# Two layers of hedgehog attention and squared-ReLU MLP: attention weights paced by POOL's copies, more row tiles turned by way of DRAM and DVE, keys taken in another order

## The chip, the cores and the metric

One core of one Trainium2 chip runs the whole program. The metric is device time in microseconds (us) for one execution; less is better.

## The reference

Two equal layers over 2048 rows of 576 floats. Each layer is a linear attention with learned feature maps (32 heads of 18), then an MLP of width 4608 with a squared ReLU; both start with a layer norm and add to the residual. All is float32.

```python
pq = einsum("bhsd,hdf->bhsf", q, w_phi); pk = einsum("bhsd,hdf->bhsf", k, w_phi)
phi_q = concatenate([softmax(pq), softmax(-pq)], axis=-1)     # phi_k alike
kv = einsum("bhsf,bhsd->bhfd", phi_k, v); z = einsum("bhsf->bhf", phi_k)
o = einsum("bhqf,bhfd->bhqd", phi_q, kv) / (einsum("bhqf,bhf->bhq", phi_q, z)[..., None] + 1e-6)
A(x) = o.reshape(B, S, D) @ wo                                # q, k, v = x @ wqkv
B(x) = square(relu(x @ w1 + b1)) @ w2 + b2
x = x + A(layernorm(x)); x = x + B(layernorm(x))              # twice, same weights
```

## The kernel before

**Products.** Every float32 operand is split into a high and a low part (float32r), and a product is three matmuls: high by high, high by low, low by high. Weights are kept in DRAM in split form and loaded from there.

**Blocks.** The rows are taken in four blocks of 512 (four tiles t of 128). The MLP of a block runs over 36 chunks f of 128 hidden features. `hidden(f)` multiplies chunk f of w1 (tile h1, rows m_2h in the profile; one load of 640 KB) with the block's turned rows into a PSUM tile ph; `square(f)` lets ACT make relu and square (hr, L980 and L981) and DVE the split (hb, L984 and L985); `second(f-1)` multiplies the chunk before with w2 (tile s2, rows m_2s, 576 KB) into accumulators (L1000 and L992). h1 and s2 have two buffers each, so the load for chunk f+1 can start when chunk f-1 has been used. In layer 0 the blocks come in the order 3, 2, 0, 1; the profile calls them m_3, m_2, m_0 and m_1. The first one also splits the MLP weights and stores them.

**What is woven in.** `g_mlp` yields between its halves: slot 2f comes after hidden(f), slot 2f+1 after second(f-1). Into these slots `weave` puts the steps of a plan: `plan.put(at, order, call)` files a call under turn `at`, and turn k falls on slot 2k+1. The steps of a block in layer 0 are:

- `plan_attend` (L868): the rest of layer 0's attention for the next block (a_2 in m_3, a_0 in m_2, a_1 in m_0): queries, division, output projection with the weights "o" (tiles a_0o0h, a_0o0l and so on), norm and turn of its rows for the MLP.
- `plan_keys` (L1515): in m_2, m_0 and m_1 the keys and values of layer 1 for the block before (n_3 in m_2, then n_2 and n_0): norm of its rows, turn, `keys(t)` with the weights k (tiles w_3k0h, w_3k0l, w_3k1h, w_3k1l), `values(t)` with the weights v (w_3v...), softmax, and `add(t)`, which adds a tile's part of kv (L593; 128 matmuls of 36 columns for two tiles). These weights come as four pieces of 720 KB each, by `asked` (L302), which returns four calls that issue them.

**Turning rows.** A product needs rows with the features on partitions. `Norm.turn` (L375) does that with four TensorE transposes a tile into PSUM (L384), then a copy by ACT (L385) and a subtraction by DVE (L386); `Norm.rest` (L389) does the last 64 features, two tiles at a time (L393 to L395). `TripNorm` (L400) does it without TensorE for the tiles in `trips`: `store` puts the normed tile into DRAM (xrm, L419; with `tails` also the last 64 features, xrt, L422), `fetch` loads it back with its 32x32 blocks exchanged (L430, L432), both issued from ACT's queue, `flip` transposes inside the blocks on DVE, and `turn` splits it with ACT (L451) and DVE (L452). In before, a_2 takes this way with tiles 0 to 2 and without tails; the other attentions of a layer take it whole; the key blocks turn all four tiles on TensorE.

**Order.** The instructions of PE, ACT, DVE and POOL stand in the order in which the program writes them. SP, which issues nearly all loads (`nc.sync.dma_start`), stands in an order that the framework's scheduler makes. Each engine takes its queue strictly from the front: a load whose buffer isn't free yet holds back all loads behind it.

Of the kernel before, what the change touches and what calls it, by code (L numbers as in the profile page):

```python
# [15 lines left out]
NT = TB // P  # L16
# [5 lines left out]
def layers_kernel(  # L22
# [278 lines left out]

    def asked(which, name, tags=TAGS_A):  # L302

        pair, calls = [], []

        def ask(half, k):
            if k == 0:
                pair.append(piece_tiles(f"{name}{which}{half}", tags))
            for d, piece in moved(which, half, k, pair[half][k]):
                nc.sync.dma_start(piece, d)  # L310

        return pair, [lambda half=half, k=k: ask(half, k) for half in range(2) for k in range(2)]
# [12 lines left out]
    class Norm:  # L325
# [49 lines left out]
        def turn(self, t):  # L375
            name, dst, xn = self.name, self.dst, self.xn.pop(t)
            if t == 0:
                dst.update(xt_tiles(name))
# [18 lines left out]
    class TripNorm(Norm):  # L397
# [44 lines left out]
        def turn(self, t):  # L442
            if t not in self.trips:
                return super().turn(t)
            xn, dst = self.xn.pop(t), self.dst
            if t == 0:
                dst.update(xt_tiles(self.name))
# [420 lines left out]
    def plan_attend(plan, at, gap, layer, b, raws, dst, name, o, homes=None, queries=None, lead=1):  # L868
# [28 lines left out]
        for t in range(NT):  # L897
            plan.put(at + t - 1, 9, out.load, t)
        trips = range(NT if whole else NT - 1)
        norm = TripNorm(dst, f"{name}n", b, out.keep, trips, whole)  # L900
        more = 0 if queries else 2
        scales = [at + 1, at + 2, at + 3, at + 4 if whole else at + 5.5 + more]
        turns = [at + more + k for k in (4, 5, 6.5, 7)]
        for t in trips:
            plan.put(scales[t] + 0.5, -1, norm.store, t)
            plan.put(at + more + t + 2.5, -1, norm.fetch, t)
            plan.put(at + more + (3.5, 4.5, 6, 6.5)[t], -1, norm.flip, t)
        plan_norm(plan, norm, out.project, [at + t for t in range(NT)], scales, turns, [at + 5 + more, at + 7 + more])

    def g_mlp(layer, b, x, after, name, fresh, apart, final):  # L910
# [66 lines left out]
        def square(f):  # L977
# [6 lines left out]
            nc.vector.tensor_copy(hh, hr)  # L984
            nc.vector.tensor_sub(hl, hr, hh.bitcast(F32))  # L985
            parts[f] = (s2, hh, hl)

# [470 lines left out]
    def body():  # L1458
# [3 lines left out]
        for layer in range(2):  # L1462
            q1 = None
            ready, prev_rows, keep = {}, None, {}
            for i, b in enumerate(order):
# [11 lines left out]
                if prev_rows is not None:  # L1477
                    at = plan_keys(plan, prev_rows, i == NB - 1, keep)
                if i + 1 < NB:
                    nb, n2 = order[i + 1], f"a{layer}_{order[i + 1]}"  # L1480
                    if i or layer:
                        o = asked("o", n2, TAGS_C)
                    if i == 0:
                        plan_attend(plan, 1, 3, layer, nb, [other.raws[t] for t in range(NT)], nxt, n2, o,
                                    TAGS_C if layer else None)
                    elif layer == 0:
# [6 lines left out]
                        for n, call in enumerate(o[1]):  # L1493
                            plan.put(at + n, 9, call)
                        plan_attend(plan, at - 4.5, 2, layer, nb, raws2, nxt, n2, o, TAGS_A, take, 2)
                    else:
                        raws2, held = [], {}
# [16 lines left out]

    def plan_keys(plan, prev_rows, last, keep):  # L1515

        pb, done = prev_rows
        m = f"1_{pb}"
        xk, es, ks, vts = {}, {}, {}, {}
        plan_norm(plan, Norm(xk, f"n{m}"), lambda t: done[t], (0, 0, 1, 2), (1, 1, 2, 3), (2, 3, 4, 4.5), (3, 5), (3,))  # L1520
        (vw, vcalls), (kw, kcalls) = asked("v", f"w{m}"), asked("k", f"w{m}", TAGS_C)
        for n in range(4):
            plan.put(8 + n if last else 2 + n / 2, 9, vcalls[n])
            plan.put(n / 2, 9, kcalls[n])
        if not last:
            for n in range(4):
                plan.put(5 + n / 2, -1, lambda n=n: spill(pb, xk, [n]))

# [16 lines left out]

        for t in range(NT):
            plan.put(4 + t, 0, keys, t)
            plan.put(5 + t, 1, soft1, t)
            plan.put(6 + t, 2, soft2, t)
            if not last:  # L1550
                plan.put(4.5 + t, 0, values, t)
                plan.put(8.5 + t // 2 * 2, 3, add, t)
        if last:
# [27 lines left out]
```

## Time and profile before

| | |
|---|---|
| median of 3 runs | 2497.05 us (2494.74 to 2499.38) |
| the profiled execution | 2497.19 us |
| its span, first to last instruction | 2495.5 us |
| PE busy | 2478.5 us, 99% |
| DVE, ACT, POOL busy | 1260.1, 788.1, 189.4 us |
| moved by DMA | 545.07 MB, 218 GB/s on the average |

The 1.7 us between span and time lie around the instructions. An engine's row in the page is its busy time, its share of the span and its instructions. In a table of waits, a row names who waited for whom: us in total, how often, the longest. A row of a timeline begins with start and duration in us; "xN" is N instructions run together; brackets at its end hold the idle time before it and what ended it. A row of a chain is start, duration and what held the end back. Durations of neighbouring matmuls overlap, so the time that one takes on PE is read from start to start.

### The profile page before, as it was taken

Reading aid. Unit: us, or ns where it says so; the run is one execution under the profiler, and the core shown is the slowest. Engines: PE = TensorE matmul, PEld = TensorE weight load, DVE = VectorE, ACT = ScalarE, POOL = GpSimd, SP = SyncE. Lnnn points to the kernel's source line nnn. Section 1 sums busy time; section 2 is a strip of 40 time slices with the busy share of each in tenths; the row PEclk is TensorE's granted clock in tenths of the full one; section 3 lists DMA queues with packets and bytes.
Section 4 is the critical chain, followed back from the end, with each engine's and each line's share of the span. In section 5 each row is a group of like instructions: output and inputs, shape, how many; then the busy total and the mean of one; then the engine's idle time right before and its main releaser. Section 6 shows DMA issues by size and latency. Waiting matters only on the chain.

```text
span 2495.5 us, 37635 instructions
## 1 busy us (share of the span) xinstructions
PE 2478.5 (99%) x14968; PEld 2182.9 (87%) x14968; DVE 1260.1 (50%) x2214; ACT 788.1 (32%) x1439; POOL 189.4 (8%) x539
## 2 busy tenths in 40 slices
PE   9999999999999999999999999999999999999999
PEld 8999888888888888888888988888888888888887
DVE  6679885545744476455113776433453436442112
ACT  5444453422232223223213332413233222312212
POOL 4211100000200001000000011000110002000000
PEclk9999999999999999999999999999999999999999
DMA  9313698986767677684565248678576867676565
GB/s 321 98 54 92 243 315 266 310 315 205 259 229 271 217 206 273 216 298 146 195 199 182 92 141 263 209 217 291 186 257 204 261 219 246 217 230 230 194 199 171
DMA packets 214374, 545.07 MB, mean 218 GB/s; under 512 B 29006, under 2 KB 96814, under 8 KB 214198
## 3 DMA queue, kind: packets, MB, share of 16 engines
q1 hardware_dynamic: 163638, 500.44, 60.8%
q10 hardware_dynamic: 50560, 42.21, 5.3%
q8 instruction: 119, 1.95, 0.3%
q14 instruction: 57, 0.47, 0.1%
HBM read 439.20 MB, written 103.38 MB: 217 GB/s over the span
## 4 chain that ended last, share of the span: by engine, by line
PE 95%; DMA 2%; DVE 1%; ACT 1%; issue 1%; SPq 0%; ACTq 0%; DVEq 0%
PE m_1ph L975 9%; PE m_3ph L975 9%; PE m_0ph L975 9%; PE m_2ph L975 9%; PE m_1acc L1000 7%; PE m_3acc L1000 7%; PE m_2acc L1000 7%; PE m_0acc L1000 7%; PE m_1acc L992 2%; PE m_3acc L992 2%; PE m_2acc L992 2%; PE m_0acc L992 2%; PE a_0po L816 1%; PE a_2po L816 1%; PE kvp L593 1%; PE a_3po L816 1%
## 5 line engine op out<-in xcount | busy, mean ns | idle before, releaser
L975 PE MATMUL m_2ph<-a_2nh,m_2h 128*128 128x512 f32 x720 | 225.2, 394 | 1.2 <-ACT m_2hr L980 0.7
L975 PE MATMUL m_0ph<-a_0nh,m_0h 128*128 128x512 f32 x720 | 225.0, 394 | 1.3 <-ACT m_0hr L980 1.1
L1000 PE MATMUL m_3acc<-m_3s,m_3hb 128*128 128x448 f32 x864 | 189.3, 367 | 0.4 <-DVE m_3hb L984 0.4
L1000 PE MATMUL m_1acc<-m_1s,m_1hb 128*128 128x448 f32 x864 | 189.0, 367 | 0.3 <-PE m_1ph L975 0.3
L1000 PE MATMUL m_2acc<-m_2s,m_2hb 128*128 128x448 f32 x864 | 188.9, 367 | 0.0
L1000 PE MATMUL m_0acc<-m_0s,m_0hb 128*128 128x448 f32 x864 | 188.8, 367 | 0.0
L984 DVE CAST m_2hb<-m_2hr 128x512 fp32r<-128x512 f32 x72 | 31.2, 433 | 292.4 <-ACT m_2hr L981 292.3
L1000 PEld LDWEIGHTS m_1acc<-m_1s,m_1hb 128*128 128x128 f32 x864 | 161.9, 188 | 18.8 <-PE m_1ph L975 0.5
L1000 PEld LDWEIGHTS m_3acc<-m_3s,m_3hb 128*128 128x128 f32 x864 | 161.2, 188 | 17.8 <-PE m_3ph L975 0.6
L1000 PEld LDWEIGHTS m_2acc<-m_2s,m_2hb 128*128 128x128 f32 x864 | 161.6, 188 | 17.2
L1000 PEld LDWEIGHTS m_0acc<-m_0s,m_0hb 128*128 128x128 f32 x864 | 161.6, 188 | 17.2
L975 PEld LDWEIGHTS m_2ph<-a_2nh,m_2h 128*128 128x128 f32 x720 | 135.3, 188 | 32.7 <-ACT m_2hr L980 1.2
L975 PEld LDWEIGHTS m_0ph<-a_0nh,m_0h 128*128 128x128 f32 x720 | 135.2, 188 | 32.8 <-ACT m_0hr L980 1.5
L984 DVE CAST m_1hb<-m_1hr 128x512 fp32r<-128x512 f32 x72 | 30.7, 427 | 258.8 <-ACT m_1hr L981 258.8
L980 ACT ACTIVATE m_2hr<-m_2ph,b1t 128x512 f32<-128x512 f32 x72 | 49.6, 689 | 339.1 <-PE m_2ph L975 327.4
L980 ACT ACTIVATE m_1hr<-m_1ph,b1t 128x512 f32<-128x512 f32 x72 | 49.6, 689 | 319.1 <-PE m_1ph L975 309.1
L980 ACT ACTIVATE m_0hr<-m_0ph,b1t 128x512 f32<-128x512 f32 x72 | 49.6, 689 | 317.2 <-PE m_0ph L975 288.6
L984 DVE CAST m_0hb<-m_0hr 128x512 fp32r<-128x512 f32 x72 | 31.5, 438 | 229.0 <-ACT m_0hr L981 229.0
L984 DVE CAST m_3hb<-m_3hr 128x512 fp32r<-128x512 f32 x72 | 31.7, 440 | 173.6 <-ACT m_3hr L981 173.6
L980 ACT ACTIVATE m_3hr<-m_3ph,b1t 128x512 f32<-128x512 f32 x72 | 49.6, 689 | 219.3 <-PE m_3ph L975 209.2
L975 PE MATMUL m_3ph<-t0onh,m_3h 128*128 128x512 f32 (+1 forms) x380 | 112.9, 384 | 0.6 <-ACT t0onh L385 0.5
L975 PE MATMUL m_1ph<-t1onh,m_1h 128*128 128x512 f32 (+1 forms) x380 | 112.4, 382 | 0.8 <-ACT t1onh L385 0.5
(2050 smaller groups left out, 5734.9 us busy)
## 6 DMA issues: line engine op xcount, KB each, us to landing
m_2h<-dw SPq DMA_DIRECT2D x72, 640.0 KB
m_0h<-dw SPq DMA_DIRECT2D x72, 640.0 KB
m_1h<-dw SPq DMA_DIRECT2D x72, 640.0 KB
m_2s<-dw SPq DMA_DIRECT2D x72, 576.0 KB
m_0s<-dw SPq DMA_DIRECT2D x72, 576.0 KB
m_1s<-dw SPq DMA_DIRECT2D x72, 576.0 KB
dw<-m_3h SPq DMA_DIRECT2D x36, 640.0 KB
m_3h<-dw SPq DMA_DIRECT2D x36, 640.0 KB
```

The source lines that it names most:

```text
L593: nc.tensor.matmul(po[32 * q : 32 * q + 32, :, j], vt[:, h * VW : h * VW + 32], e[:, :, h * DH : (h + 1) * DH], start=not stay, stop=True, ...
L816: nc.tensor.matmul(pt[:, :HP], a, m[:w, g], start=(g == 0 and k == 0), stop=(g == NG - 1 and k == 2))
L975: nc.tensor.matmul(ph[:, cols], a, m, start=(k == 0), stop=(k == 3 * KC + 1))
L980: nc.scalar.activation(hr, ph, AF.Relu, bias=b1t[:, f : f + 1])
L984: nc.vector.tensor_copy(hh, hr)
L992: nc.tensor.matmul(acc[KC], a, m, start=(f == 0 and k == 0), stop=(f == NF - 1 and k == 2))
L1000: nc.tensor.matmul(acc[t][:, :R], a[:, rows], m, start=(f == 0 and k == 0), stop=(f == NF - 1 and k == 2))
```

## The change

1. `asked` gets a switch `paced`. With it, POOL first copies one element of the newest hr (`beat["now"]`, set at the end of `square`) into the piece's tile, and only then is the piece's load issued: the load overwrites that element, so it must come behind the copy, and the copy behind hr. It is used for k, v and "o" in layer 0's blocks (32 copies; of "o" only the pieces of 126 partitions are held so).
2. `plan_attend` sends all four tiles and the tails by way of DRAM also for a_2.
3. `plan_keys` turns tiles 0 and 1 by way of DRAM (store at turn 2, fetch at 3 and 4, flip at 4.5 and 5.5, turn at 5 and 6), tiles 2 and 3 on TensorE at turns 2 and 3, and all tails on TensorE. Keys and values go in the order 2, 3, 0, 1. The adds of the second pair move from turn 10.5 to 11.5, the spills from 5 + n/2 to 6 + n/2.
4. The weights k of the next key block are asked for in the block before, at the last four chunks (`keyw`); the weights v follow at turns 0 to 3. For the first key block, in m_2, k comes at turns 0 to 1.5 and v at 2 to 3.5, as in the code before; for the last v comes at 8 to 11.

```diff
--- before.py
+++ after.py
@@ -299,13 +299,17 @@
                 nc.sync.dma_start(d.rearrange("p (h c n) -> p h c n", h=2, c=NC)[:w, :, g],
                                   piece.rearrange("p (h n) -> p h n", h=2))
 
-    def asked(which, name, tags=TAGS_A):
+    beat = {}
+
+    def asked(which, name, tags=TAGS_A, paced=False):
 
         pair, calls = [], []
 
         def ask(half, k):
             if k == 0:
                 pair.append(piece_tiles(f"{name}{which}{half}", tags))
+            if paced:
+                nc.gpsimd.tensor_copy(pair[half][k][0:1, 0, 0:1], beat["now"][0:1, 0:1])
             for d, piece in moved(which, half, k, pair[half][k]):
                 nc.sync.dma_start(piece, d)
 
@@ -374,7 +378,7 @@
 
         def turn(self, t):
             name, dst, xn = self.name, self.dst, self.xn.pop(t)
-            if t == 0:
+            if not dst:
                 dst.update(xt_tiles(name))
             xh, xl = dst["h"], dst["l"]
             rows = slice(t * P, (t + 1) * P)
@@ -443,7 +447,7 @@
             if t not in self.trips:
                 return super().turn(t)
             xn, dst = self.xn.pop(t), self.dst
-            if t == 0:
+            if not dst:
                 dst.update(xt_tiles(self.name))
             rows = slice(t * P, (t + 1) * P)
             src = xn.rearrange("p (g b r) -> p b g r", g=KC, b=KC)
@@ -896,12 +900,11 @@
         at += NG + 1
         for t in range(NT):
             plan.put(at + t - 1, 9, out.load, t)
-        trips = range(NT if whole else NT - 1)
-        norm = TripNorm(dst, f"{name}n", b, out.keep, trips, whole)
-        more = 0 if queries else 2
-        scales = [at + 1, at + 2, at + 3, at + 4 if whole else at + 5.5 + more]
+        norm = TripNorm(dst, f"{name}n", b, out.keep, range(NT), True)
+        more = 0 if queries else 2 if whole else 4
+        scales = [at + 1, at + 2, at + 3, at + 4]
         turns = [at + more + k for k in (4, 5, 6.5, 7)]
-        for t in trips:
+        for t in range(NT):
             plan.put(scales[t] + 0.5, -1, norm.store, t)
             plan.put(at + more + t + 2.5, -1, norm.fetch, t)
             plan.put(at + more + (3.5, 4.5, 6, 6.5)[t], -1, norm.flip, t)
@@ -983,6 +986,7 @@
             hh, hl = hb[:, :TB], hb[:, TB : 2 * TB]
             nc.vector.tensor_copy(hh, hr)
             nc.vector.tensor_sub(hl, hr, hh.bitcast(F32))
+            beat["now"] = hr
             parts[f] = (s2, hh, hl)
 
         def features(f):
@@ -1460,7 +1464,7 @@
         order = [NB - 1, NB - 2] + list(range(NB - 2))
         queries, other, o, last_keys = opening()
         for layer in range(2):
-            q1 = None
+            q1 = keyw = None
             ready, prev_rows, keep = {}, None, {}
             for i, b in enumerate(order):
                 n = f"{layer}_{b}"
@@ -1475,11 +1479,11 @@
                         plan.on(2 + t, 0, out.keep, t, out.x[t])
                 at = 0
                 if prev_rows is not None:
-                    at = plan_keys(plan, prev_rows, i == NB - 1, keep)
+                    at = plan_keys(plan, prev_rows, i == NB - 1, keep, keyw)
                 if i + 1 < NB:
                     nb, n2 = order[i + 1], f"a{layer}_{order[i + 1]}"
                     if i or layer:
-                        o = asked("o", n2, TAGS_C)
+                        o = asked("o", n2, TAGS_C, not layer)
                     if i == 0:
                         plan_attend(plan, 1, 3, layer, nb, [other.raws[t] for t in range(NT)], nxt, n2, o,
                                     TAGS_C if layer else None)
@@ -1493,6 +1497,9 @@
                         for n, call in enumerate(o[1]):
                             plan.put(at + n, 9, call)
                         plan_attend(plan, at - 4.5, 2, layer, nb, raws2, nxt, n2, o, TAGS_A, take, 2)
+                        keyw = asked("k", f"w1_{b}", TAGS_C, True)
+                        for n, call in enumerate(keyw[1]):
+                            plan.put(at + 20.5 + n, 9, call)
                     else:
                         raws2, held = [], {}
                         for k in range(4):
@@ -1512,19 +1519,26 @@
                 queries, other, o, last_keys = between(rows, keep)
                 order = [order[-1], order[-2]] + order[:2]
 
-    def plan_keys(plan, prev_rows, last, keep):
+    def plan_keys(plan, prev_rows, last, keep, keyw):
 
         pb, done = prev_rows
         m = f"1_{pb}"
         xk, es, ks, vts = {}, {}, {}, {}
-        plan_norm(plan, Norm(xk, f"n{m}"), lambda t: done[t], (0, 0, 1, 2), (1, 1, 2, 3), (2, 3, 4, 4.5), (3, 5), (3,))
-        (vw, vcalls), (kw, kcalls) = asked("v", f"w{m}"), asked("k", f"w{m}", TAGS_C)
+        norm = TripNorm(xk, f"n{m}", pb, None, range(2), False)
+        for t in range(2):
+            plan.put(2, -1, norm.store, t)
+            plan.put(3 + t, -1, norm.fetch, t)
+            plan.put(4.5 + t, -1, norm.flip, t)
+        plan_norm(plan, norm, lambda t: done[t], (0, 0, 0.5, 1), (0.5, 0.5, 1, 1.5), (5, 6, 2, 3), (3.5, 3))
+        vw, vcalls = asked("v", f"w{m}", TAGS_A, True)
+        kw, kcalls = keyw or asked("k", f"w{m}", TAGS_C, True)
         for n in range(4):
-            plan.put(8 + n if last else 2 + n / 2, 9, vcalls[n])
-            plan.put(n / 2, 9, kcalls[n])
+            plan.put(8 + n if last else n if keyw else 2 + n / 2, 9, vcalls[n])
+            if not keyw:
+                plan.put(n / 2, 9, kcalls[n])
         if not last:
             for n in range(4):
-                plan.put(5 + n / 2, -1, lambda n=n: spill(pb, xk, [n]))
+                plan.put(6 + n / 2, -1, lambda n=n: spill(pb, xk, [n]))
 
         def keys(t):
             ks[t] = make_raw(xk, t, kw, f"k{m}k")
@@ -1543,13 +1557,13 @@
         def add(t):
             kv_tile(1, vts.pop(t), es.pop(t), f"kv{m}_{t}")
 
-        for t in range(NT):
-            plan.put(4 + t, 0, keys, t)
-            plan.put(5 + t, 1, soft1, t)
-            plan.put(6 + t, 2, soft2, t)
+        for n, t in enumerate((2, 3, 0, 1)):
+            plan.put(4 + n, 0, keys, t)
+            plan.put(5 + n, 1, soft1, t)
+            plan.put(6 + n, 2, soft2, t)
             if not last:
-                plan.put(4.5 + t, 0, values, t)
-                plan.put(8.5 + t // 2 * 2, 3, add, t)
+                plan.put(4.5 + n, 0, values, t)
+                plan.put(8.5 + n // 2 * 3, 3, add, t)
         if last:
             keep.update(x=xk, es=es, v=vw, k=kw)
         return 11.5
```

SP's queue at the start of block m_2, before. m_2h_3 is h1 of chunk 3, m_2s_2 is s2 of chunk 2, w_3k and w_3v are the weight pieces; w_3k0l, w_3k0h, w_3k1h and w_3v0h stand earlier, in m_3.

```order
L938 DMA m_2h_3_6339<-dw_3_144 128x1280
L950 DMA m_2s_2_6318<-dw_2_179 128x1152
L310 DMA w_3k1l<-kept_kl 128x1440
L938 DMA m_2h_4_6403<-dw_4_145 128x1280
L310 DMA w_3v0l<-kept_vl 128x1440
L950 DMA m_2s_3_6378<-dw_3_180 128x1152
L310 DMA w_3v1h<-kept_vh 128x1440
L938 DMA m_2h_5_6462<-dw_5_146 128x1280
L950 DMA m_2s_4_6442<-dw_4_181 128x1152
L310 DMA w_3v1l<-kept_vl 128x1440
L938 DMA m_2h_6_6543<-dw_6_147 128x1280
```

And now, from the same load on:

```order
L941 DMA m_2h_3_6354<-dw_3_144 128x1280
L314 DMA w_3k0h<-kept_kh 128x1440
L953 DMA m_2s_2_6320<-dw_2_179 128x1152
L314 DMA w_3k0l<-kept_kl 128x1440
L314 DMA w_3k1h<-kept_kh 128x1440
L314 DMA w_3k1l<-kept_kl 128x1440
L953 DMA m_2s_3_6397<-dw_3_180 128x1152
L314 DMA w_3v0h<-kept_vh 128x1440
L941 DMA m_2h_4_6414<-dw_4_145 128x1280
L314 DMA w_3v0l<-kept_vl 128x1440
L953 DMA m_2s_4_6454<-dw_4_181 128x1152
L314 DMA w_3v1h<-kept_vh 128x1440
```

All eight pieces of w_3 now stand here, and m_2h_4 has moved from behind m_2s_2 and one piece to behind m_2s_3 and five.

SP's queue at the end of block m_2, before. w_2k are the weights k for the next key block, xm and m_2x the residual rows (the pieces of w_2v stand above this place).

```order
L310 DMA w_2k0l<-kept_kl 128x1440
L824 DMA xm_2_87<-a_0x_8325 128x576
L310 DMA w_2k0h<-kept_kh 128x1440
L950 DMA m_2s_32_8572<-dw_32_209 128x1152
L1062 DMA m_2x_8778<-xm_3_96 128x576
L310 DMA w_2k1h<-kept_kh 128x1440
L938 DMA m_2h_34_8635<-dw_34_175 128x1280
L950 DMA m_2s_33_8627<-dw_33_210 128x1152
L824 DMA xm_3_88<-a_0x_8417 128x576
L938 DMA m_2h_35_8682<-dw_35_176 128x1280
L310 DMA w_2k1l<-kept_kl 128x1440
L950 DMA m_2s_34_8677<-dw_34_211 128x1152
```

And now:

```order
L941 DMA m_2h_34_8650<-dw_34_175 128x1280
L314 DMA w_2k0h<-kept_kh 128x1440
L953 DMA m_2s_33_8638<-dw_33_210 128x1152
L828 DMA xm_3_88<-a_0x_8428 128x576
L941 DMA m_2h_35_8699<-dw_35_176 128x1280
L314 DMA w_2k0l<-kept_kl 128x1440
L953 DMA m_2s_34_8692<-dw_34_211 128x1152
L941 DMA m_0h_0_8832<-dw_0_141 128x1280
L314 DMA w_2k1h<-kept_kh 128x1440
L953 DMA m_2s_35_8738<-dw_35_212 128x1152
L941 DMA m_0h_1_8857<-dw_1_142 128x1280
L314 DMA w_2k1l<-kept_kl 128x1440
```

The pieces of w_2k have moved back, the second half of them to both sides of the last m_2s, and the pieces of w_2v have gone to the start of the next block.

PE's order in m_2 ahead of the first keys of n_3, before. m_2acc are the accumulators of second(3), n_3p the PSUM tiles of the transposes, k_3kp the keys.

```order
L1000 MATMUL m_2acc_6298<-m_2s_3_6378,m_2hb_6423 128x448 x3
L1000 MATMUL m_2acc_6299<-m_2s_3_6378,m_2hb_6423 128x448 x3
L992 MATMUL m_2acc_6300<-m_2hb_6423,m_2s_3_6378 128x512 x3
L384 MATMUL n_3p_6503<-ident,n_3n_6392 128x128 x4
L493 MATMUL k_3kp_6511<-w_3k0h,n_3h 128x288
L493 MATMUL k_3kp_6511<-w_3k0l,n_3h 128x288
L493 MATMUL k_3kp_6511<-w_3k0h,n_3l 128x288
```

And now:

```order
L978 MATMUL m_2ph_6476<-a_2nh,m_2h_4_6414 128x512 x3
L397 MATMUL n_3p_6499<-ident,n_3e 64x128 x2
L1004 MATMUL m_2acc_6298<-m_2s_3_6397,m_2hb_6434 128x448 x3
L1004 MATMUL m_2acc_6299<-m_2s_3_6397,m_2hb_6434 128x448 x3
L1004 MATMUL m_2acc_6300<-m_2s_3_6397,m_2hb_6434 128x448 x3
L1004 MATMUL m_2acc_6301<-m_2s_3_6397,m_2hb_6434 128x448 x3
L996 MATMUL m_2acc_6302<-m_2hb_6434,m_2s_3_6397 128x512 x3
L497 MATMUL k_3kp_6522<-w_3k0h,n_3h 128x288
L497 MATMUL k_3kp_6522<-w_3k0l,n_3h 128x288
```

The group of four transposes ahead of the keys is gone, and the group of two for the tails has left its place behind a group of four and stands by itself ahead of second(3).

## The prediction

> **What bounds the kernel now.** I read the page first: its share of each engine, then the chain that ended last.
>
> ```profile
> span 2495.5 us, 37635 instructions
> PE 2478.5 (99%) x14968; PEld 2182.9 (87%) x14968; DVE 1260.1 (50%) x2214; ACT 788.1 (32%) x1439; POOL 189.4 (8%) x539
> PE 95%; DMA 2%; DVE 1%; ACT 1%; issue 1%; SPq 0%; ACTq 0%; DVEq 0%
> ```
>
> PE is busy for 99% of the span and holds 95% of the chain; DVE, ACT and POOL have room on the average. So the time moves only by work that PE gains or loses, and by the few places where PE stands still. Next I read PE's waits in layer 0 after the opening.
>
> ```profile
> PE kv_3k L593 <- issue: 1.2, 1, 1.2
> PE m_0ph L975 <- ACT m_0hr L980: 1.1, 1, 1.1
> PE m_2ph L975 <- ACT m_2hr L980: 0.7, 1, 0.7
> PE m_2ph L975 <- DMA m_2h<-dw: 0.5, 1, 0.5
> PE m_0ph L975 <- DMA m_0h<-dw: 0.2, 1, 0.2
> ```
>
> These five single waits, 3.7 us together, are the only ones of size in the stretch that the change touches. Whatever it does to stalls is bounded by them on the side of a gain.
>
> **Transposes taken from PE.** The change turns tiles 0 and 1 of the three key blocks (n_3, n_2, n_0) through DRAM: two groups of four transposes fewer in each. In a_2 it takes away what was still on PE, a group of two and one of six. The timeline of PE gives their price.
>
> ```profile
> 461.89 0.38 PE L393 MATMUL a_2np<-ident,a_2ne 128*64 128x128 f32 x2
> 462.03 1.26 PE L1000 MATMUL m_3acc<-m_3s,m_3hb 128*128 128x448 f32 x5
> ...
> 474.86 0.60 PE L384 MATMUL a_2np<-ident,a_2nn 128*128 128x128 f32 x4
> 475.29 0.38 PE L393 MATMUL a_2np<-ident,a_2ne 128*64 128x128 f32 x2
> 475.43 0.65 PE L1000 MATMUL m_3acc<-m_3s,m_3hb 128*128 128x448 f32 x2
> ...
> 536.61 0.60 PE L384 MATMUL n_3p<-ident,n_3n 128*128 128x128 f32 x4
> 536.97 0.48 PE L975 MATMUL m_2ph<-a_2nh,m_2h 128*128 128x512 f32 x1
> 537.29 0.40 PE L975 MATMUL m_2ph<-a_2nl,m_2h 128*128 128x512 f32 x1
> ```
>
> Durations overlap, so starts count: four transposes hold PE from 536.61 to 536.97, 0.36 us. The matmul behind them takes 0.32 to the next start. The chain has the ordinary step:
>
> ```profile
> 606.82 3.27 PE m_2ph L975 x14
> ```
>
> 3.27 / 14 = 0.23, so each switch costs 0.09 more, and a group of four 0.45. The six of a_2 take 0.57 + 0.09, the two 0.14 + 0.09: 0.89. Sum: 3 x 2 x 0.45 + 0.89 = 3.6 us off PE, with nothing beside it that could hide it, since PE was not waiting there. Their two tails (L393) stay on PE in the key blocks, as groups of six and of two; splitting a group costs 0.09 and I leave it in the rounding.
>
> [...]
>
> What replaces them runs beside PE: DVE's block transposes and ACT's copy.
>
> ```profile
> 786.27 1.13 ACT L451 ACTIVATE a_0nh<-a_0nn 128x512 fp32r<-128x512 f32 x1
> ...
> 791.41 0.69 ACT L980 ACTIVATE m_2hr<-m_2ph,b1t 128x512 f32<-128x512 f32 x1 [4.00 <-PE m_2ph L975]
> ```
>
> ACT's copy of a fetched tile takes 1.13 us, and ACT then idles 4.00 us for PE: hidden, costed at nothing. If that cover were gone, it would delay one relu by 1.1 us at most. Keys in the order 2, 3, 0, 1 give the two tiles through DRAM two keys' time more.
>
> **Stalls that may go.** The two waits for m_2h and m_0h come from the weights "o" of the next attention, loaded at 594 to 610 ahead of m_2h:
>
> ```profile
> 594.81 0.33 SPq L310 DMA_DIRECT2D a_0o0h<-kept_oh  x1
> ...
> 610.50 0.39 SPq L310 DMA_DIRECT2D a_0o1l<-kept_ol  x1
> ```
>
> ```profile
> 610.11 11.37 DMA m_2h<-dw
> ```
>
> 11.37 us for one load of 640 KB. The change holds the large pieces back until about chunk 12 to 15, one a chunk, so both waits should go: 0.7 us. The two waits for ACT are a fetch (L430) that stands in ACT's queue, ahead of relu (L980), until a store has landed:
>
> ```profile
> 789.04 10.64 DMA xrm<-a_0nr
> ...
> 799.77 0.34 ACTq L430 DMA_DIRECT2D a_0nn<-xrm  x1
> 800.21 0.60 ACTq L432 DMA_DIRECT2D a_0ne<-xrt  x1
> 800.86 0.69 ACT L980 ACTIVATE m_2hr<-m_2ph,b1t 128x512 f32<-128x512 f32 x1 [6.62 <-issue]
> ```
>
> The store crawls beside w_2k and m_2s. The change holds w_2k's four pieces for hr(32) to hr(35), one a chunk, and moves w_2v out of the block altogether. The store need only land 1 to 2 us sooner, so I take all of 1.8 us. But the last piece but one now stands ahead of the last m_2s on SP:
>
> ```profile
> 801.06 0.58 SPq L950 DMA_DIRECT2D m_2s<-dw  x1
> ```
>
> A piece of 720 KB moves in 1.9 us at the 398 GB/s of the table below; between nothing and 1 us of that reaches second(35). I take 0.4 at each of two block ends, 0.8 lost. The wait at kv_3k has no releaser in the profile. It falls in a run of 128 matmuls of 36 columns; the add moves by one turn, into a stretch without the "o" loads. It may go wholly or come back elsewhere (six such adds, one wait): 0.8 of 1.2. Together 0.7 + 1.8 + 0.8 - 0.8 = 2.5 us regained, between 0 and 3.7.
>
> **The new wait.** SP issues in order, and the start of m_2 now has all eight pieces of w_3k and w_3v in it; before, four had come in m_3. Where m_2h_4 stood second behind m_2s_2 it now stands behind m_2s_3 (rows in the section on the change). SP and PE in before:
>
> ```profile
> 527.23 0.32 SPq L938 DMA_DIRECT2D m_2h<-dw  x1
> 530.39 0.32 SPq L950 DMA_DIRECT2D m_2s<-dw  x1
> ...
> 533.67 0.32 SPq L938 DMA_DIRECT2D m_2h<-dw  x1
> ...
> 536.80 0.32 SPq L950 DMA_DIRECT2D m_2s<-dw  x1
> ```
>
> ```profile
> 544.01 0.47 PE L975 MATMUL m_2ph<-a_2nh,m_2h 128*128 128x512 f32 x1
> ```
>
> m_2h_4 went out at 533.67 (its buffer was then free) and was needed at 544.0. Now m_2s_3 must go first, which waits for second(1): 536.8, and m_2h_4 follows at about 537.6. In the ring from m_2h_3 on lie two h, two s and five pieces.
>
> ```profile
> m_2h<-dw SPq DMA_DIRECT2D x3, 640.0 KB
> m_2s<-dw SPq DMA_DIRECT2D x3, 576.0 KB
> w_3k1l<-kept_kl SPq DMA_DIRECT2D x1, 720.0 KB
> ```
>
> ```profile
> 530.00:535.00 5.00, 5.00 (x24) 4.15 (x23) 4.08 (x13) 1.29 (x2) 2.00 (x6) 1.00 0.80 282
> 535.00:540.00 5.00, 5.00 (x26) 4.18 (x25) 3.22 (x7) 0.62 (x2) 0.52 (x1) 1.00 1.02 398
> 540.00:545.00 5.00, 5.00 (x28) 4.41 (x27) 1.62 (x4) 2.18 (x4) 1.28 (x10) 1.00 0.93 320
> 545.00:550.00 5.00, 5.00 (x25) 4.34 (x24) 2.67 (x6) 1.32 (x2) 0.00 (x0) 1.00 0.88 323
> 610.00:620.00 10.00, 10.00 (x169) 8.84 (x169) 9.09 (x14) 4.63 (x7) 0.00 (x0) 1.00 0.99 251
> ```
>
> That is 6.18 MB, and two stores of a tile (128 x 512 x 4 bytes each) add 0.52. The last two columns are the DMA share and GB/s. I let the ring start on it at 529, an estimate: 1.8 us behind the issue at 527.23. At 398 GB/s without the stores m_2h_4 lands at 529 + 15.5 = 544.5; at 331, the mean of the four rows from 530 to 550, with the stores, at 529 + 20.2 = 549.2. PE waits 0.5 to 5.2 us; I take 2.8, about the middle, since the queue is full here as in the second row but the stores trickle. A row speaks for less: before, four pieces passed here without a wait.
>
> [...]
>
> In m_0 and m_1 the k pieces have come in the block before, so only four v pieces stand at the start, one a chunk: I cost nothing, up to 1 us each. The 32 one-element copies run on POOL, which is 8% busy. A copy that waits for hr(f) holds back n_3d (the norms' root) behind it, hidden by the four chunks before the first transposes; without that cover the keys would slip by one chunk's relu, 1 us.
>
> **Sum.** The profiled execution took 2497.19 us (1.7 around its span), 0.14 above the median of 2497.05. 2497.2 - 3.6 - 2.5 + 2.8 = 2493.9; against the median 2493.8. A gain of 3.3 us is 0.13%; 0.2%, about what a measurement of this kernel can tell from no change, is 5.0 us (2492.1 and 2502.0).
>
> **Rivals.**
> - *Nothing new waits.* The ring clears w_3 by 544.0, and all 3.7 us come back: 2497.1 - 3.6 - 3.7 = 2489.8. For it: the lower bound above is only 0.5 late. Against: SP's order, which puts the issue of m_2h_4 4 us later.
> - *The fetches go on holding ACT.* More tiles now go by store and fetch, and at m_2's start the store lies beside a full queue as at 789. If the two old waits stay and two like them come (1.8 us): 2497.1 - 3.6 - 0.7 - 0.8 + 2.8 + 1.8 = 2496.6, no change. [...] Against: two chunks lie between store and fetch.
> - *The start of m_2 jams.* If the ring with small store rows in it moves only 251 GB/s, as from 610 to 620, 6.7 MB take 26.7 us, m_2h_4 lands at 555.7 and PE waits 11.7: 2497.1 - 3.6 - 2.5 + 11.7 = 2502.7, slower. The gains of 6.1 us are used up from a landing at 550.1, a rate of 318 GB/s; 0.2% is lost from 555, 258 GB/s. Against: 282 was the lowest row here, and PE had no load to wait for then.
>
> **How the numbers follow.** Forecast 0.54 (2491 to 2497), nothing new waits 0.22, fetches hold ACT 0.15, jam 0.09. Faster by over 0.2%: nearly all of the second and a fifth of the first, 0.32. Slower: most of the jam, 0.07. Between: 0.61. The range from 2489 to 2499 leaves out the jam and the edges of the others.
>
> **What would show it.** Right: no L388 group on a_2; n_3p, n_2p and n_0p in layer 0's blocks with half as many; a wait of PE for m_2h of 1 to 5 us near 547; no wait of m_2ph and m_0ph for ACT at the block ends, none for m_2h or m_0h in the middle of the blocks. Wrong in the new wait, if hidden(4) of m_2 starts on time; wrong in the regained stalls, if m_2ph or m_0ph still waits for ACT, or m_2acc for m_2s at the end. A wait of k_3kp for n_3h would mean that the trips are late.

## The result

The changed kernel takes 2511.9 us (2510.91 to 2520.35, 4 runs), the kernel before 2496.68 us in the same rounds: a ratio of 1.0068, 95% interval 1.0044 to 1.0091. It is slower by some 15 us, where 2493.8 was forecast and the range ended at 2499. Single runs of experiments 2, 4 and 12 came at a granted clock of 0.85 or less and took at least 7% longer; they are left out of all figures, and the kernel of 12, whose profile was such a run, was profiled again as 14.

Three lines of the page of the changed kernel, for the three shown of before:

```profile
span 2509.2 us, 37703 instructions
PE 2478.8 (99%) x14936; PEld 2179.7 (87%) x14936; DVE 1271.0 (51%) x2223; ACT 791.4 (32%) x1439; POOL 197.6 (8%) x571
PE 93%; DMA 3%; DVE 2%; issue 1%; ACT 1%; POOL 0%; ACTq 0%; DVEq 0%; SPq 0%; POOLq 0%
```

PE has 32 instructions fewer, as planned, and nowhere waits for the rows turned by way of DRAM, but its share of the chain fell from 95% to 93%. The span grew by 13.7 us, so PE stands still for longer. Its waits in the blocks that the change touches:

```profile
PE m_2ph L978 <- DMA m_2h<-dw: 6.1, 1, 6.1
PE m_0ph L978 <- ACT m_0hr L983: 2.9, 2, 1.8
PE m_2acc L1004 <- DVE m_2hb L987: 2.7, 3, 1.4
PE m_2acc L996 <- DVE a_0nh L467: 2.1, 1, 2.1
PE m_0acc L1004 <- DVE m_0hb L987: 1.2, 2, 0.8
PE m_2ph L978 <- ACT m_2hr L983: 1.0, 1, 1.0
PE m_0acc L996 <- DMA m_0s<-dw: 0.9, 1, 0.9
```

16.9 us against 3.7 before. The wait at kv_3k is gone, and so are the two short waits for m_2h and m_0h in the middle of the blocks. Three other places have come up.

**The start of m_2.** PE stands for 6.06 us ahead of hidden(4), and goes on slowly. Its timeline, its chain, and four stretches (the last three columns are the granted clock, the DMA share and GB/s):

```profile
542.99 0.38 PE L397 MATMUL n_3p<-ident,n_3e 128*64 128x128 f32 x2
549.43 0.77 PE L978 MATMUL m_2ph<-a_2nh,m_2h 128*128 128x512 f32 x1 [6.06 <-DMA m_2h<-dw]
```

```profile
539.89 9.41 DMA m_2h<-dw
...
549.43 3.67 PE m_2ph L978 x9
```

```profile
543.00:546.00 3.00, 0.37 (x4) 0.10 (x1) 1.11 (x2) 0.86 (x2) 0.00 (x0) 0.93 1.02 423
546.00:549.00 3.00, 0.00 (x0) 0.00 (x0) 0.00 (x0) 0.00 (x0) 0.00 (x0) 0.50 1.02 418
549.00:552.00 3.00, 2.57 (x6) 2.12 (x7) 0.00 (x0) 0.00 (x0) 0.00 (x0) 0.50 1.02 421
552.00:555.00 3.00, 3.00 (x15) 2.46 (x15) 0.00 (x0) 0.66 (x1) 0.00 (x0) 0.93 0.77 312
```

m_2h_4 went out at 539.89 and landed at 549.30, on a ring at 418 to 423 GB/s. While PE stood, its granted clock fell to 0.50 and stayed there until after 552: 3.67 / 9 = 0.41 us a matmul instead of 0.23. About 1.5 us go there, on top of the wait.

**The middle of m_2 and m_0.** The chain from 660 to 681:

```profile
660.22 13.80 DMA phs<-a_0z
...
674.47 1.18 ACT a_0Q3e L557
...
675.67 1.36 DVE a_0r L560
...
677.61 1.22 DVE a_0m L853
...
678.89 1.24 issue
680.12 0.43 DVE m_2hb L987
```

A store of phs (the attention's way to turn its features through DRAM) takes 13.80 us. The fetch behind it holds ACT's queue; ACT's and DVE's softmax steps come late, and with them hb, for which PE waits. In m_0 it is 14.4 us. Before, these stores landed 4.4 to 6.2 us after their issue.

**The ends of m_2 and m_0.** Here the forecast had waits going. They have grown:

```profile
798.69 10.14 DMA xrt<-a_0nr
...
809.62 0.70 ACT m_2hr L983
```

```profile
1104.67 0.69 ACT L983 ACTIVATE m_0hr<-m_0ph,b1t 128x512 f32<-128x512 f32 x1 [7.65 <-DMA xrt<-a_1nr]
1106.08 0.43 POOL L312 CAST w_0k1h<-m_0hr 1x1 fp32r<-1x1 f32 x1 [10.05 <-ACT m_0hr L984]
1106.54 0.32 SPq L314 DMA_DIRECT2D w_0k1h<-kept_kh  x1
1106.95 0.38 SPq L953 DMA_DIRECT2D m_0s<-dw  x1
```

```profile
1106.95 5.93 DMA m_0s<-dw
```

At the end of m_2 the store still takes 10.14 us. At the end of m_0 the last m_0s stands on SP behind a piece of w_0k, that piece behind its copy on POOL, and the copy behind a late hr: a relu that ACT issued late because of the fetch holds back a load that has nothing to do with it.

At the end of m_2 the table of waits names the wrong releaser. The matmul that waits 2.1 us there, until 819.06, reads only hb and s2. Its hb was ready at 817.3; its s2 stands on SP right behind the piece w_2k1h (issued at 811.50), and the last completion signal of this load came at 818.93, 0.04 us before DVE finished a_0nh:

```profile
811.91 0.39 SPq L953 DMA_DIRECT2D m_2s<-dw  x1
```

So both block ends wait for the last s2, 3.0 us together, and for ACT, 2.8 us.

### The profile page after: what moved, and what is told of

Read it like the earlier page. It is cut to its first block, busy times and chain, and to the rows that moved or that the text cites. A ratio compares the mean times of both kernels' runs of the same rounds, so it can differ in the third digit from the quotient of the medians.

```text
span 2509.2 us, 37703 instructions
## 1 busy us (share of the span) xinstructions
PE 2478.8 (99%) x14936; PEld 2179.7 (87%) x14936; DVE 1271.0 (51%) x2223; ACT 791.4 (32%) x1439; POOL 197.6 (8%) x571
## 4 chain that ended last, share of the span: by engine, by line
PE 93%; DMA 3%; DVE 2%; issue 1%; ACT 1%; POOL 0%; ACTq 0%; DVEq 0%; SPq 0%; POOLq 0%
PE m_3ph L978 9%; PE m_1ph L978 9%; PE m_2ph L978 8%; PE m_0ph L978 8%; PE m_3acc L1004 7%; PE m_1acc L1004 7%; PE m_2acc L1004 6%; PE m_0acc L1004 6%; PE m_1acc L996 2%; PE m_3acc L996 2%; PE m_2acc L996 2%; PE m_0acc L996 2%; PE a_0po L820 1%; PE a_2po L820 1%; PE kvp L597 1%
## 5 line engine op out<-in xcount | busy, mean ns | idle before, releaser
L978 PE MATMUL m_2ph<-a_2nl,m_2h 128*128 128x512 f32 x288 | 113.3, 394 | 0.0
```

What stands on the lines that cost most here:

```text
L978: nc.tensor.matmul(ph[:, cols], a, m, start=(k == 0), stop=(k == 3 * KC + 1))
```

## The experiments

All ratios are to the kernel before, in rounds of their own, with a 95% interval. Differences in us are those of medians. The ratio of the changed kernel is itself known only to 0.24%, 6 us, so a difference of 5 us to it says little without the waits in the profile beside it.

**1. First key block unpaced.**

```diff
-        vw, vcalls = asked("v", f"w{m}", TAGS_A, True)
-        kw, kcalls = keyw or asked("k", f"w{m}", TAGS_C, True)
+        vw, vcalls = asked("v", f"w{m}", TAGS_A, bool(keyw))
+        kw, kcalls = keyw or asked("k", f"w{m}", TAGS_C)
```

> The changed kernel, with the weights of the first key block (w_3k and w_3v) no longer paced; SP then has four of the eight pieces ahead of block m_2 again and m_2h_4 behind m_2s_2 and one piece. Theory (SP's order at the start of m_2 made m_2h_4 late): the wait of PE for m_2h of 6.1 us near 549 and the matmuls at half clock behind it are gone, about 7.9 us less than the changed kernel, some 2504 us; the waits near 670, 970 and at the block ends stay. Rival (the stores of the two tiles share the ring and make m_2h late, whatever the order): a wait for m_2h of 3 us or more stays near 545 to 549, and the gain is under 4 us.

2507.3 us, 1.0042 (1.0029 to 1.0054): 4.6 us less than the changed kernel, not 7.9. In the start of m_2 one wait is left, at 529, for m_2h_2:

```profile
PE m_2ph L978 <- DMA m_2h<-dw: 1.9, 1, 1.9
```

The stores of the tiles are still there, and m_2h_4 is in time. So the paced pieces make the wait, by their place in SP's queue or by their copies, and not the stores; experiments 8 and 9 part the two. The 1.9 us fall where four pieces of w_3 now come in m_3's end, beside a_2's stores. A wait of 1.2 to 1.9 us stands there in every profile with the trips and w_3 unpaced (experiments 1, 4 to 7, 10 and 11) and in before there is none; so the trips bring it.

**2. The pieces of o unpaced.**

```diff
-                        o = asked("o", n2, TAGS_C, not layer)
+                        o = asked("o", n2, TAGS_C)
```

> The changed kernel, with the weights o of the next attention no longer paced, so that they load ahead of the time when the phs stores run. Theory (the held-back pieces slow the phs stores, and ACT stands at the fetch behind them): the stores of phs land in 4 to 6 us instead of 10 to 14, the waits of m_2acc and m_0acc for hb near 660 to 680 and 965 to 975 (6.6 us together by starts) go, the two waits for m_2h and m_0h in the middle of the blocks (1.0 us) come back: about 5 us less than the changed kernel, some 2507 us. Rival (the tiles by way of DRAM overload ACT and DVE): the waits for hb stay, the time within 2 us of the changed kernel.

2505.0 us, 1.0031 (1.0019 to 1.0044): 6.9 us less. The phs stores land in 4.6 to 6.0 us, and no wait for hb is left. The tiles through DRAM do not overload ACT or DVE; the rival falls.

**3. No early k.** w_2k, w_2v, w_0k and w_0v are asked for unpaced in their own blocks (the lines of `plan_keys` that do this are left out here).

```diff
-                        keyw = asked("k", f"w1_{b}", TAGS_C, True)
-                        for n, call in enumerate(keyw[1]):
-                            plan.put(at + 20.5 + n, 9, call)
```

> The changed kernel, without the early, paced load of the next key block's k: w_2k, w_2v, w_0k, w_0v are asked for unpaced in their own block as before (the first key block and o stay paced). Theory (the held-back k pieces come on top of the last trips and of the last m_2s): the waits at the ends of m_2 and m_0 (1.2 + 2.2 and 1.9 + 1.1 us) shrink to those of before (0.9 and 1.3): 3 to 4 us less than the changed kernel, some 2508 us. Rival (these waits belong to the stores of the trips and come whatever is loaded): they stay within 1 us of the changed kernel's.

2511.4 us, 1.0050 (1.0036 to 1.0064). The waits at the block ends did shrink, from 5.8 us to 2.6:

```profile
PE m_2ph L978 <- ACT m_2hr L983: 0.8, 1, 0.8
PE m_0ph L978 <- ACT m_0hr L983: 1.5, 1, 1.5
PE m_0acc L996 <- DVE m_0hb L988: 0.3, 1, 0.3
```

But the time did not follow: the waits in the middle were longer in its profile (3.5 us for m_2hb alone, against 2.7), which is that of its slowest run. Its runs lie between 2506.3 and 2512.9. The loss varies by several us from run to run, enough to hide this gain; that it did is argued, not shown.

**4. The trips alone.** Nothing paced, no early k; a_2, the key blocks and the order of the keys as in the changed kernel.

> The kernel before with the trips alone: a_2 whole by way of DRAM, tiles 0 and 1 of the key blocks by way of DRAM, keys in the order 2, 3, 0, 1; nothing paced, weights asked for as before. Theory (the loss is the pacing's, the transposes taken from PE are worth their 3.5 us): 3 to 4 us less than before, 2492.5 to 2494, with the five waits of before. Rival (the trips cost more than they save): no gain, or slower than before.

2494.3 us, 0.9989 (0.9980 to 0.9998): 2.7 us less than before. The part of the change that the forecast was surest of holds; the price of four transposes on PE was near: in the profile PE's waits in these blocks are 0.8 us longer than before and the span is 2.8 us shorter, which leaves 3.6 for the transposes. The whole loss is the pacing's and the early k's.

**5. Early k alone, with the trips.** Experiments 1 and 2 together.

> The changed kernel with both the first key block's weights and o unpaced; of the pacing only the early k and the v of the second and third key block are left. Theory (three separate losses that add): the wait for m_2h near 549 and the waits for hb in the middle go as in the two runs before, about 11 us less than the changed kernel, 2501; the block ends keep 3 to 4 us more than with the trips alone, which took 2494.3. Rival (the ends cost nothing by themselves, as the run without the early k had suggested): within 2 us of the trips alone.

2498.2 us, 1.0006 (0.9997 to 1.0015). 4.6 and 6.9 us of experiments 1 and 2 make 11.5; together they gave 13.7, which the intervals do not tell apart. Against the trips alone the early k, with the paced v that goes with it, costs 3.9 us. In the profile, which is of one of its slower runs (2500.88), PE's waits at the block ends are 6.4 us, against 2.3 with the trips alone. At the end of m_0:

```profile
PE m_0acc L996 <- DMA m_0s<-dw: 2.7, 1, 2.7
PE m_0ph L978 <- ACT m_0hr L983: 1.6, 1, 1.6
```

**6 and 7. The trips with o paced, at the changed kernel's turns and two and a half turns earlier.**

```diff
-                            plan.put(at + n, 9, call)
+                            plan.put(at - 2.5 + n, 9, call)
```

> The trips alone, with the pieces of o paced as in the changed kernel (chunks 12 to 15). Theory: phs lands in 10 to 14 us again, waits for hb near 665 and 965, 5 to 7 us more than the trips alone: 2499 to 2501. Rival (the middle of the blocks suffers only after the late start of m_2): within 2 us of the trips alone.

> The same with the four calls of o two and a half turns earlier, so that the pieces come before the first store of phs. Theory (not the copy but the place of the load beside phs costs): phs lands in 4 to 7 us, no waits for hb, and the waits of m_2h and m_0h in the middle stay away as well: 2493 to 2495, as the trips alone or 1 us less. Rival (POOL's copies and the queue behind them cost by themselves): 3 us or more above the trips alone.

2506.0 us, 1.0032 (1.0019 to 1.0044), and 2494.7 us, 0.9990 (0.9981 to 0.9999). Same copies, same loads, same POOL: 11 us lie between them, more than the 6.9 of experiment 2. Waits of PE from 940 to 975 in the first, whose profile is of its fastest run (2499.66) and so shows only a part:

```profile
PE m_0acc L1004 <- DVE m_0hb L987: 1.9, 2, 1.1
PE m_0ph L978 <- ACT m_0hr L983: 1.8, 1, 1.8
```

The second has neither, and no wait for m_2h or m_0h in the middle. Its phs stores took up to some 9 us, not the 4 to 7 of the forecast, but PE waited for none of what follows them. Here the paced loads, moved away from these stores, cost nothing that can be measured.

**8. Pacing and early k alone.** The kernel before with these two; no new trips.

> The kernel before with the pacing and the early k alone, no new trips, keys in the old order; SP's order at the start of m_2 is that of the changed kernel, and no store of row tiles stands beside it. Theory: nearly all of the loss is here, 2512 to 2516; without the two stores PE waits for m_2h 1 to 2 us less than 6.1. Rival (the new trips and the pacing hurt each other): under 2505.

2518.0 us, 1.0085 (1.0071 to 1.0098), 2 us above the forecast: in the middle PE waits up to 3.4 us for hb, and works at half clock behind it (0.50 from 673.80 and from 974.16 on), which with the start of m_2 (0.50 from 547.50 to 550.92) costs at least 6.5 us in this profile, an estimate: half of PE's 13.0 us of work in these stretches up to 680 and 980. SP's order at the start of m_2 is that of the changed kernel; no store stands beside it:

```profile
PE m_2ph L979 <- DMA m_2h<-dw: 3.2, 1, 3.2
```

The order alone makes 3.2 us, and m_2h_4 left at 537.72 (forecast: 537.6). That 3.2 is close to the 2.8 of the forecast is partly luck: the forecast counted two stores, which are not here. Its slow rate of 331 GB/s without them gives 529 + 18.7 = 547.7, and hidden(4) started at 547.52. Why was the wait 6.1 in the changed kernel? Its SP and POOL:

```profile
534.80 0.32 SPq L314 DMA_DIRECT2D w_3k1h<-kept_kh  x1
538.03 0.32 SPq L314 DMA_DIRECT2D w_3k1l<-kept_kl  x1
538.44 0.88 SPq L953 DMA_DIRECT2D m_2s<-dw  x1
539.41 0.38 SPq L314 DMA_DIRECT2D w_3v0h<-kept_vh  x1
539.89 0.74 SPq L941 DMA_DIRECT2D m_2h<-dw  x1
```

```profile
536.51 0.28 POOL L363 TENSOR_SCALAR n_3d<-n_3m 128x1 f32<-128x1 f32 x1 [1.74 <-DVE n_3m L362]
536.87 0.99 POOL L364 TENSOR_TENSOR n_3d<-n_3d,mhalf 128x1 f32<-128x1 f32 x1
537.83 0.17 POOL L312 CAST w_3k1l<-m_2hr 1x1 fp32r<-1x1 f32 x1
```

The copy for w_3k1l waits on POOL behind the root of tile 3's norm, and that for DVE's statistics. m_2h_4, two loads further on, stands behind it.

**9. The norm of tile 3 one turn later.**

```diff
-... (0, 0, 0.5, 1), (0.5, 0.5, 1, 1.5), (5, 6, 2, 3), (3.5, 3))
+... (0, 0, 0.5, 2), (0.5, 0.5, 1, 2.5), (5, 6, 2, 3), (3.5, 3))
```

> The changed kernel, with the norm of tile 3 of the key blocks one turn later (statistics at turn 2, scaling at 2.5), so that on POOL the copies for w_3k1l and w_3v0h stand ahead of that tile's root instead of behind it; SP's order stays. Theory (POOL's queue held the copy for w_3k1l until 537.8 and with it m_2h_4 until 539.9, which made 2 of the 6.1 us): m_2h_4 goes out at 537 to 538, PE waits 3.5 to 4.5 us, and with the shorter stretch at half clock 2 to 3 us less than the changed kernel, 2509. Rival (the ring is full anyway and an earlier issue lands no earlier): the wait stays at 5.5 us or more.

```profile
PE m_2ph L978 <- DMA m_2h<-dw: 2.6, 1, 2.6
```

The wait fell from 6.1 to 2.6, further than expected. m_2h_4 left 17.2 us after the block's first matmul, as in experiment 8 (17.1), where it had been 20.2 in the changed kernel. So POOL's queue made over half of the wait, and the two stores, which are here again, add nothing to it. The time is 2515.6 us, 1.0068 (1.0054 to 1.0081): nothing of that reached the end. In this profile the waits for hb in the middle are 1.7 us longer than in the changed kernel's, with phs stores of up to 18 us, and half clock behind one of them (0.50 from 674.08 to 677.50) costs another 1.7, an estimate; that the later norm makes this is not shown. Behind the short wait at the start, too, the clock stood at 0.50 from 547.79 to 551.20.

**10 and 11. Early k three turns sooner; and the same with o paced early.** The first is the kernel of experiment 5 with `at + 17.5 + n` for `at + 20.5 + n`, the second also has the diff of 7.

> The run with the early k alone (2498.2), with these loads three turns earlier (held for hr of chunks 29 to 32 or by their buffers, if these come free later). Theory (what costs 4 us at the block ends is the place beside the last stores of the trips and the last m_2s): about 2495 to 2496, and the wait of the last chunk for m_2s and m_0s gone. Rival (k loaded a block early costs in any place): 2498 or more.

> The trips, o paced two and a half turns earlier, and k three turns earlier, the first key block unpaced. Theory (the copies do no harm where the load has no latecomer beside it): 2492 to 2496, as the trips alone or a little less. Rival (paced loads cost even so): 2498 or more.

2498.7 us, 1.0000 (0.9991 to 1.0009), and 2495.7 us, 0.9988 (0.9979 to 0.9997). By the first the early k costs in any place: the waits for m_2s and m_0s fell from 3.7 us to 0.7, but a wait for ACT of 2.6 came at the end of m_0, and behind it the clock stood at 0.50 from 1090.65 to 1094.06 (last section), by estimate some 1.4 us more in this profile. The second, with the same early k, does as well as the trips alone. The two intervals overlap, so what the early k costs by itself stays open.

**12 and 14. The phs stores by SP.** The changed kernel with `nc.sync.dma_start(phs...` for `nc.scalar`; run twice.

> The changed kernel, with the stores of phs issued by SP instead of ACT, so that they stand in the loads' own ring (q1) instead of beside it (q10). Theory (beside a full q1 each DMA engine gives the two queues turns packet by packet: a phs packet of 640 bytes, 32 ns, waits for a q1 packet of 4 to 5 KB, 200 ns; 64 packets an engine for two stores make 15 us): in the loads' ring the stores land in 5 to 9 us instead of 11 to 14, the waits for hb near 670 and 970 shrink by half or more, 3 to 6 us less than the changed kernel, 2506 to 2509. Rival (the deferred pieces of o simply fill the ring, and any store waits as long): they land in 11 us or more and the time stays within 2 us.

> The changed kernel with the phs stores issued by SP once more, for a profile at full clock. It took as long as the changed kernel. Theory (turns between the queues): the phs stores do land in 5 to 9 us and the waits for hb are gone or small, and the time is lost elsewhere, since SP now waits for phs data ahead of m_2h and m_2s. Rival (a full ring): the stores land in 11 us or more and the waits for hb are those of the changed kernel.

2513.0 us, 1.0068 (1.0054 to 1.0082): no gain, as the rival had it. In the profile of the second run the stores land 9.3 to 11.2 us after their issue in the crowded stretches, neither as theory nor as rival had it, and PE waits for other things. Its waits from 655 to 685 and from 955 to 985:

```profile
PE m_2acc L1004 <- DMA m_2s<-dw: 1.5, 1, 1.5
PE m_2ph L978 <- DMA m_2h<-dw: 1.0, 1, 1.0
```

```profile
PE m_0acc L1004 <- DMA m_0s<-dw: 2.4, 2, 1.3
PE m_0ph L978 <- DMA m_0h<-dw: 1.5, 1, 1.5
```

No wait for hb is left, and the weights wait instead. Both explanations hold a part: the queue that the stores stand in decided who was late, hb for 3.9 us in the changed kernel's middle and the weights for 6.4 us here, but with o held back to these chunks the DMA engines are full: from 658 to 680 q1 took 85.3% of their time and q10 17.0%.

**13. The stores of the trips by SP, on the trips alone.**

```diff
-            nc.scalar.dma_start(xrm[self.b][t]...
+            nc.sync.dma_start(xrm[self.b][t]...       # and xrt likewise
```

> The trips alone, with the stores of xrm and xrt issued by SP, in the loads' own ring. Theory (the same taking of turns makes the stores at the block ends slow): they land in under 8 us where they took up to 10.6 to 11.0, the waits for ACT at the ends of m_2 and m_0 (1.5 and 0.9 us) go, 1 to 2 us less than the trips alone. Rival (in the loads' ring a store that waits for its data holds back the loads behind it): 2 us or more slower than the trips alone.

2491.3 us, 0.9981 (0.9972 to 0.9990), 3.0 less than the trips alone. In the stretch where these stores took 10.4 to 11.2 us they land in 6.0 to 6.5, and the waits of m_2ph and m_0ph for relu at the block ends are gone. PE now holds 97% of the chain, against 96% with the trips alone. At m_2's start the wait of 1.2 us at 529 is gone; one of 0.9 for m_2h has come at 536, and one of 0.8 for the turned rows n_3h at 544.

**15. The same with o paced early.**

> The trips with xrm and xrt stored by SP (2491.3), and o paced two and a half turns early. Theory: the waits for m_2h and m_0h in the middle of the blocks (0.7 and less) go as well: 2490 to 2491.5. Rival (the copies cost by themselves): 2493 or more.

2492.3 us, 0.9980 (0.9971 to 0.9989), between theory and rival: no different from 13, though the waits for m_2h and m_0h in the middle did go. Both are faster than the kernel before and the changed one.

## Why the prediction was wrong

- **What bounds the kernel: right**, and incomplete. PE's waits before bound what can be regained. Nothing bounded what could be lost, and the range treated the losses as if something did.
- **Transposes off PE, 3.6 us: about right.** The trips alone gained 2.7 (0.5 to 5.0 by the interval), with a new wait of 1.2 for m_2h at m_2's start set against it. In the changed kernel itself m_3 and m_1, where PE's idle time stayed the same within 0.1 us, became 0.7 and 1.0 us shorter (forecast 0.9 each). DVE's and ACT's work stayed hidden, as costed.
- **Stalls in the middle, "both waits should go: 0.7 us": this step failed first.** They went. But the step asked only what the pieces were moved away from, and not what they were moved next to: at chunks 12 to 15 the phs stores begin, from ACT's queue. That cost 6.9 us (experiment 2) to 11 (6 against 7), where the forecast had a gain of 0.7.
- **Stalls at the block ends, "I take all of 1.8 us", less 0.8: failed.** They grew from 1.8 to 5.8 us: 2.8 for ACT, where nothing was to be left, and 3.0 for the last s2, where 0.8 was costed. The held-back w_2k stands just as close to the last stores as before (10.14 us for the one that ACT waits for, against 10.64), and a copy that waits for hr ties SP's queue to ACT's delays. By medians the early k costs 3.9 us (experiment 5 against 4; experiments 10 and 11 leave its share open). The waits for ACT that are left without the early k go when these stores change their queue (experiment 13); with the early k this was not tried.
- **The new wait at m_2's start: the mechanism was right, the size was not.** Forecast 2.8 us, bounds 0.5 to 5.2, measured 6.1, and some 1.5 of slow clock behind it. SP's order alone gave 3.2 (experiment 8), and the stores, which the upper bound counted, nothing that shows (9 against 8). The missing term was POOL's queue, and the text had it the wrong way round: it said that a copy holds back n_3d, and costed that at nothing; n_3d, behind DVE, held back the copy. The clock was no term at all.
- **Rivals.** The jam at m_2's start named the right place and the wrong price; that fetches hold ACT named part of the other two. That all three come together was not among the cases, and slower got 0.07.
- **Left over.** By PE's table of waits 13.2 us came and 3.6 went, with 1.5 for the clock: 11.1 of the 13.7 us of span. Counted from the first hidden matmul of one block to that of the next, m_2 grew by 11.7 us and m_0 by 3.9, so the remaining 2.6 lie inside these two; what makes them is open. Why the runs of one kernel differ by several us is open in part: the clock has a share. The changed kernel's run of 2520.35 has a mean granted clock of 0.996 and the three others 0.998; in experiment 6 the two fastest runs have 1.000, the others 0.998 and 0.999.

## What to carry to other kernels

When a load is held back, look at the time it moves to: who else uses the ring there, and who waits for that. A copy that paces a load ties three queues together, its own engine's, the load's, and that of whatever it waits for; each takes the worst delay of the others (here m_2h_4 left at 539.89, behind a copy that POOL could run only at 537.83, behind a norm that waited for DVE). Where a store of small rows stands beside a full stream of large loads and someone waits for it, try it in the loads' own queue before moving the loads; it gained 3.0 us for the row tiles, and nothing for phs, where the DMA engines were full (85.3 and 17.0% for the two queues). And price a wait of the full engine with the clock that it may lose: in these traces a wait of 2.6 us cost nothing more (experiment 9, from 972.57) or some 1.4 us (experiment 10), and one of 3.4 us at least 2.4 (experiment 8, from 671.65), estimates from PE's work at 0.50.

## What the hardware showed unexpectedly

From 664 to 674 of the changed kernel two DMA queues, q1 with loads and q10 with phs stores, shared the engines by packets, not by bytes (packets, MB, share):

```profile
q1 hardware_dynamic: 692, 3.02, 83.4%
q10 hardware_dynamic: 631, 0.40, 13.2%
```

Nearly one packet for one packet, 692 against 631, and 7.6 times the bytes for the queue with large ones. Two stores of phs are 1024 packets of 640 bytes, 64 for each of 16 engines if they are spread evenly. By these rows a q1 packet occupied an engine for about 193 ns and a q10 packet for about 33. If each phs packet waits for one of q1, 64 x 0.226 = 14.5 us, an estimate; the pair took 14.3 (from the first issue at 659.76 to the last landing at 674.02). Experiment 12 put the stores among the loads and gained nothing (2513.0 us): the sharing decided who was late, and no time came back.

Where both ends of a stretch at 0.50 can be read, PE's clock stood there for 3.41 us or twice that: 6.83 us in the changed kernel (545.58 to 552.41), 3.4 and 3.4 in experiment 9 (from 547.79 and from 674.08), 3.4 in experiment 1 (from 963.50), 6.8 and 3.4 in experiment 2 (from 547.58 and from 1107.36). In experiment 9 the two begin 126.29 us apart, 37 x 3.413, and in experiment 2 559.78, 164 x 3.413. Cut into slices of that length, counted from such a beginning, two waits of nearly the same length come apart. One of 2.61 us in experiment 10, from 1088.71:

```profile
1087.24:1090.65 3.41, 1.47 (x7) 0.94 (x5) 0.00 (x0) 0.07 (x1) 0.00 (x0) 1.00 0.32 92
1090.65:1094.06 3.41, 2.74 (x7) 2.16 (x8) 1.74 (x3) 1.54 (x3) 0.00 (x0) 0.50 0.94 336
```

And one of 2.64 us in experiment 9, from 972.57:

```profile
971.04:974.45 3.41, 1.53 (x7) 0.97 (x6) 0.00 (x0) 1.03 (x1) 0.00 (x0) 1.00 0.52 152
974.45:977.86 3.41, 2.65 (x12) 2.19 (x13) 3.18 (x4) 1.34 (x3) 0.00 (x0) 1.00 0.89 323
```

PE stood for 1.94 us of the first slice of one, and the clock was halved; for 1.88 us of the first slice of the other, and it was not. Other slices at full clock that half the clock followed had 1.98 us of idle (experiment 9, 670.67 to 674.08), 2.21 (the changed kernel, 542.17 to 545.58) and 2.3 (experiment 2, 1103.95 to 1107.36). Of the changed kernel's slices from 200 us on that full clock followed, the two with the most idle had 1.72 (1101.96 to 1105.38) and 1.64 (815.24 to 818.65). So in these traces the place where the slices cut a wait decided whether it cost more: of PE's work at 0.50 about half was lost (0.41 us a matmul against 0.23), by estimate 1.4 us in the second slice of experiment 10 (2.74 / 2), and nothing in that of experiment 9. A rule beyond these slices is not shown.
